# Weight preparation spread over 33 units, two blocks interleaved, and a rearranged chain after the last unit

## The chip, the core and the metric

The program runs on one core of a Trainium2 chip. The metric is the device time of one execution in microseconds. In what follows PE is the TensorE, DVE the VectorE, ACT the ScalarE, POOL the GpSimd and SP the queue from which all transfers here are issued.

## The reference

```python
x = block-causal attention of q, k, v          # 4 batches, 8 heads, 576 tokens, head size 64; blocks of 64
x = x.transpose(0, 2, 1, 3).reshape(2304, 512)
h = x @ w_in                                   # 512 -> 2048; w_in and w_out are float64 in memory
g = where(h >= 1, h, where(h <= -1, 0, (h + 1) ** 2 / 4))
y = g @ w_out                                  # 2048 -> 512
logits = y @ phi                               # 32 slots
d = softmax of logits over the 2304 tokens     # dispatch
s = d.T @ y                                    # 32 x 512, 4 slots to each of 8 experts
slot_out[e] = relu(s[e] @ w1[e]) @ w2[e]       # 512 -> 1024 -> 512
return (softmax of logits over the 32 slots) @ slot_out
```

All results are float32. The weights w1 and w2 of the experts are 33.6 MB together, the output is 4.7 MB.

## The kernel before, in words

There are three stages.

**Attention** (`attention`, `Pair`) handles 16 pairs of heads, one after another and overlapped, by the table PLAN. Its steps w0, w1 and w2 prepare the first READY = 6 of 16 tiles of w_in meanwhile, half a tile for each pair. The result x stays on the chip, in blocks of tokens BLK (512, 512, 512, 512, 256), blocks 0 and 1 already as a high and a low part, 2 to 4 as they are.

**The units** (`Moe.run`): unit (b, f) forms 128 columns f of h for block b, by 12 matmuls of 128x128 weights against 512 tokens (`h_unit`: high by high, high by low, low by high; 256 tokens in block 4), into one of three PSUM buffers of the pool ptr. Then `act_unit` forms the gate g; it is DVE's L520 that reads h last and so frees the buffer. The loop runs over 80 units k = 16 b + f. In unit k the tile READY + k is prepared as well, one a unit until 32 tiles are done (16 of w_in, 16 of w_out, in units 0 to 25): `w_raw` loads the float64 words, `w_mul` is an ACT pass (L422), `w_bits` four DVE passes (L428 to L431), `w_parts` POOL's work (L446 and L447 for w_in, the single addition L439 for w_out, which is then stored to DRAM, `wod`).

Beside this the table `sides` puts further steps behind a unit: `wo_turn` transposes a tile of w_out (PE L460, copied out by ACT), `wo_phi` and `wo_back` turn four of them into w2p = w_out phi; `quad` transposes four columns of g to gn (L534) and adds their logits (L540), each of the last in one of four 32-row groups of the array; `soft`, `disp`, `slots` and `weigh` do the softmax over tokens block by block, with a running maximum (`e.nm`) and scaled sums S. Each of these steps takes one of two PSUM buffers of the pool psc, or of ptr. `feed` issues 72 pieces of the experts' weights (32 of w1, 40 of w2) from SP as soon as one of 47 slots of 4 KB per partition (pools b4 and c4) is free by a plan, which a dry run of the same code makes.

**The end**: `chain` is the last quad, the softmax of block 4, the maximum and sums over all row groups (`maximum`, `weights`), the slots' inputs (`slots`, `turn`, `inputs`, `spread`); `tail` holds the experts' matmuls (`w1`, line L844; `w2`, line L871) and the output. The engines run each their instructions in the written order; a wait holds up everything behind it on its engine. `e.copy("A", ...)` is ACT, "D" is DVE.

Of the kernel before, what the change touches and what calls it, by code (L numbers as in the profile page):

```python
# [7 lines left out]
F32 = mybir.dt.float32  # L8
# [228 lines left out]
READY = 6  # L237
# [65 lines left out]
class Moe:  # L303


    BLK = [(0, 512), (512, 512), (1024, 512), (1536, 512), (2048, 256)]
    ASIDE = 2
    CAP = {"b4": 27, "c4": 20}

    def __init__(self, e, nc, live=None):  # L310
# [26 lines left out]
    def room(self, key):  # L337
# [46 lines left out]
    def split(self, i):  # L384

        n = self.BLK[i][1]
        for u in range(n // 256):
# [5 lines left out]
            yield one  # L393

# [57 lines left out]
    def wo_turn(self, f):  # L452
# [5 lines left out]
        ps = e.psc.tile([P, 2, 512], F32, tag="sc", name=f"wt{f}")[:, 0].rearrange("p (k c) -> p k c", k=4)  # L458
# [34 lines left out]
    def h_unit(self, b, f):  # L493
# [29 lines left out]
    def quad(self, b, q):  # L523
# [3 lines left out]
        nj = n // P  # L527
        fs = range(4 * q, 4 * q + 4)
        for u in range(nj // 2):
            ps = e.psc.tile([P, 2, 512], F32, tag="sc", name=f"gn{b}{q}{u}")  # L530
            for a in range(2):
                o = (2 * u + a) * P
                for i, f in enumerate(fs):
                    nc.tensor.transpose(ps[:, a, i * P:(i + 1) * P], self.gt(b, f)[:, o:o + P], e.ident)  # L534
            self.gn[b, q, u] = ps
        if q == 0:
            self.lt = e.ppv.tile([P, 512], F32, tag="pv", name=f"lt{b}")
# [4 lines left out]
        a = 1024 // n  # L542
        self.drop(*[f"g{b}_{f}" for f in fs if f % a == 0])
        for u in range(nj // 2):
            t = self.new([P, 2, 512], F32, f"gn{b}{q}{u}")
            e.copy("A", t, self.gn[b, q, u])
            self.gn[b, q, u] = t


    def soft(self, b):  # L550
        e, nc, sp = self.e, self.nc, self.e.sp
        R = self.BLK[b][1] // 4
        lt = self.lt[0:R, 0:P]
# [3 lines left out]
        nm, l = e.nm[0:R], e.l[0:R]  # L557
        if b == 0:
            nc.vector.tensor_reduce(out=nm, in_=lt, axis=AX.X, op=ALU.max, negate=True)
            nc.scalar.activation(E[0:R], lt, AF.Exp, bias=nm, accum_out=l)  # L560
        else:
            bm = sp.tile([P, 3], F32, tag="bm", bufs=2, name=f"bm{b}")
            f, rs = bm[0:R, 1:2], bm[0:R, 2:3]
            v["f"] = f
            nc.vector.tensor_reduce(out=bm[0:R, 0:1], in_=lt, axis=AX.X, op=ALU.max, negate=True)
            nc.vector.tensor_tensor(out=bm[0:R, 0:1], in0=bm[0:R, 0:1], in1=nm, op=ALU.min)
            nc.scalar.activation(E[0:R], lt, AF.Exp, bias=bm[0:R, 0:1], accum_out=rs)
            nc.scalar.activation(f, nm, AF.Exp, bias=bm[0:R, 0:1], scale=-1.0)
# [489 lines left out]
```

## Time and profile before

| | us |
|---|---|
| median of 2 runs | 561.64 (561.08 to 562.2) |
| the profiled execution | 561.42 |
| its span, first to last instruction | 559.6 |
| PE busy | 511.5 (91%) |
| DVE busy | 344.2 (62%) |
| ACT busy | 319.9 (57%) |
| POOL busy | 196.7 (35%) |
| read from and written to memory | 68.75 MB and 8.91 MB |

The span is what the rows cover; the execution lasts 1.8 us longer. Shares are means over stages with different limits, so rows are read by stage: attention to about 182 us, units from there to 489 us, of these the ones with preparation to about 300 us, then chain and tail.

### The profile page before, as it was taken

The numbers are of one execution on the slowest core, as the hardware profiler recorded it, in microseconds if no ns is written. First come the engines' busy times: TensorE is split into PE (matmuls) and PEld (weight loads), VectorE is DVE, ScalarE is ACT, GpSimd is POOL, SyncE is SP. The second block draws the span as 40 slices with busy tenths as digits, with TensorE's granted clock in tenths as the row PEclk, the third lists the DMA queues.
The fourth block names the chain that finished last, engine by engine and source line by source line (L and its number), as shares of the span: only waits on it lengthen the run. The fifth ranks groups of instructions, "written<-read, shape, count | busy, mean of one in ns | idle before, by whom it ended". The sixth has DMA issues, their size and how long they took to land.

```text
span 559.6 us, 11650 instructions
## 1 busy us (share of the span) xinstructions
PE 511.5 (91%) x4492; PEld 387.9 (69%) x4492; DVE 344.2 (62%) x679; ACT 319.9 (57%) x723; POOL 196.7 (35%) x255
## 2 busy tenths in 40 slices
PE   6899999999998976787989999999999999989995
PEld 5687777777776754565768867678868887943354
DVE  7799998997764899878652523344454446431232
ACT  5799988987863867577776433434324343320132
POOL 5888888887651566423220200003000100000000
PEclk8799999999999999999999999999999999989999
DMA  4542542523314522365520000142620059659998
GB/s 148 141 138 77 158 122 77 168 69 101 87 27 143 216 81 76 126 213 186 169 97 1 2 1 2 39 151 76 222 79 1 1 194 368 211 205 358 409 412 327
DMA packets 39542, 79.45 MB, mean 142 GB/s; under 512 B 8384, under 2 KB 17728, under 8 KB 39488
## 3 DMA queue, kind: packets, MB, share of 16 engines
q1 hardware_dynamic: 39488, 78.72, 41.3%
q8 instruction: 35, 0.57, 0.4%
q14 instruction: 19, 0.16, 0.1%
HBM read 68.75 MB, written 8.91 MB: 139 GB/s over the span
## 4 chain that ended last, share of the span: by engine, by line
PE 55%; DVE 22%; ACT 10%; issue 4%; DMA 3%; POOL 2%; SPq 0%; DVEq 0%; POOLq 0%; ACTq 0%
PE h L501 25%; PE gn L534 5%; ACT pr L147 5%; DVE wab L429 4%; DVE nm L142 3%; PE lt L540 3%; PE s L587 3%; DMA raw<-in_w_out_dram 3%; PE om L184 3%; PE eh L844 3%; PE acc L871 2%; DVE wab L428 2%; DVE PT L248 2%; DVE g L520 2%; DVE sm L152 1%
## 5 line engine op out<-in xcount | busy, mean ns | idle before, releaser
L501 PE MATMUL h<-xh,w 128*128 128x512 f32 (+1 forms) x384 | 108.9, 362 | 0.0
L501 PE MATMUL h<-xt,w 128*128 128x512 f32 x384 | 95.0, 398 | 13.0 <-DVE g L520 12.9
L158 POOL TENSOR_SCALAR pr<-pr,sm 128x384 f32<-128x384 f32 (+2 forms) x144 | 85.8, 614 | 22.0 <-DVE sm L153 10.5
L501 PEld LDWEIGHTS h<-xt,w 128*128 128x128 f32 x384 | 70.0, 188 | 31.5 <-DVE g L520 17.4
L519 DVE SCALAR_TENSOR_TENSOR ga<-ga 128x512 f32<-128x512 f32 (+1 forms) x52 | 34.2, 658 | 93.6 <-ACT ga L518 93.6
L518 ACT ACTIVATE ga<-h,half 128x512 f32<-128x512 f32 (+1 forms) x52 | 32.4, 622 | 97.0 <-PE h L501 96.2
L147 ACT ACTIVATE pr<-sc,nm 128x512 f32<-128x512 f32 (+2 forms) x144 | 79.0, 564 | 14.0 <-DVE nm L142 9.1
L501 PEld LDWEIGHTS h<-xh,w 128*128 128x128 f32 x384 | 68.5, 189 | 18.4 <-issue 8.0
L501 PE MATMUL h<-xl,w 128*128 128x512 f32 (+1 forms) x192 | 68.2, 355 | 0.0
L520 DVE TENSOR_TENSOR g<-h,ga 128x512 f32<-128x512 f32 (+1 forms) x80 | 51.0, 637 | 27.9 <-ACT ga L516 25.3
L614 POOL TENSOR_TENSOR cn<-cn,cm 128x128 f32<-128x128 f32 (+1 forms) x5 | 2.2, 442 | 186.2 <-DVE cm L613 186.2
L142 DVE TENSOR_REDUCE nm<-sc 128x2 f32<-128x1024 f32 (+1 forms) x64 | 51.7, 816 | 3.9 <-PE sc L123 3.5
L120 PE MATMUL sc<-K,Q 64*128 64x512 f32 (+3 forms) x384 | 47.2, 360 | 3.6 <-ACT pr L147 2.8
L246 ACT COPY gn<-gn 128x1024 f32<-128x1024 f32 x36 | 35.2, 1012 | 11.9 <-PE gn L534 10.5
L120 PEld LDWEIGHTS sc<-K,Q 64*128 64x128 f32 x384 | 29.8, 193 | 14.0 <-ACT pr L147 7.2
L501 PEld LDWEIGHTS h<-xl,w 128*128 128x128 f32 x192 | 36.3, 189 | 4.5
L534 PE MATMUL gn<-ident,g 128*128 128x128 f32 x288 | 35.5, 274 | 2.1 <-DVE g L520 1.2
L534 PEld LDWEIGHTS gn<-ident,g 128*128 128x128 f32 x288 | 32.1, 140 | 6.3 <-issue 1.7
L439 POOL TENSOR_TENSOR wab<-wab 128x512 f32<-128x512 f32 x16 | 20.5, 1282 | 44.2 <-DVE wab L431 41.8
L429 DVE SCALAR_TENSOR_TENSOR wab<-wab 128x512 uint32<-128x512 uint32 (+1 forms) x38 | 32.9, 865 | 2.2
L446 POOL TENSOR_TENSOR wab<-wab,w 128x256 f32<-128x256 f32 (+1 forms) x22 | 24.9, 1132 | 25.7 <-PE h L501 13.1
L422 ACT ACTIVATE wab<-raw 128x512 f32<-128x512 f32 (+1 forms) x38 | 22.7, 599 | 19.1 <-DMA raw<-in_w_out_dram 11.9
(192 smaller groups left out, 891.8 us busy)
## 6 DMA issues: line engine op xcount, KB each, us to landing
ew<-in_w_dram SPq DMA_DIRECT2D x32, 512.0 KB, 4.6
raw<-in_w_in_dram SPq DMA_DIRECT2D x16, 512.0 KB, 4.7
raw<-in_w_out_dram SPq DMA_DIRECT2D x16, 512.0 KB, 3.7
ew<-in_w2a_dram SPq DMA_DIRECT2D x16, 510.0 KB, 8.3
ew<-in_w2b_dram SPq DMA_DIRECT2D x16, 344.0 KB, 6.8
kn<-in_k_dram SPq DMA_DIRECT2D x16, 288.0 KB, 3.7
qn<-in_q_dram SPq DMA_DIRECT2D x16, 288.0 KB, 3.2
vn<-in_v_dram SPq DMA_DIRECT2D x16, 256.0 KB, 3.4
```

Source lines behind the costliest of these rows:

```text
L120: nc.tensor.matmul(sc[:, h, 0:n], self.Q[r, qa, 128 * i:128 * i + 128], self.K[r, ka, 0:n], start=(k == 0), stop=False)
L142: nc.vector.tensor_reduce(out=self.negm[:, 2 * i:2 * i + 2], in_=self.scs[i][:, :, 0:128 * (i + 1)], axis=AX.X, op=ALU.max, negate=True)
L147: self.nc.scalar.activation(pr, sc, AF.Exp, bias=self.negm[:, b:b + 1], accum_out=self.sums[:, b:b + 1])
L158: self.nc.gpsimd.tensor_scalar(out=pr, in0=pr, scalar1=self.sums[:, b:b + 1], scalar2=1.0, op0=ALU.mult, op1=ALU.mult)
L246: nc.scalar.copy(dst, src)
L429: v.scalar_tensor_tensor(out=Au, in0=Au, scalar=3, in1=Bu, op0=ALU.logical_shift_left, op1=ALU.bitwise_or)
L446: p.tensor_tensor(out=A, in0=A, in1=w[:, 0].bitcast(F32), op=ALU.subtract)
L501: nc.tensor.matmul(ph[:, 0:n], w[:, wi, kk], self.x(b, kk, xi)[:, 0:n], start=(m == 0), stop=(m == 11))
L518: nc.scalar.activation(ga, ph, AF.Relu, bias=e.half[:, 0:1], scale=0.5)
L519: nc.vector.scalar_tensor_tensor(out=ga, in0=ga, scalar=1.0, in1=ga, op0=ALU.min, op1=ALU.mult)
L520: nc.vector.tensor_tensor(out=g, in0=ph, in1=ga, op=ALU.max)
L534: nc.tensor.transpose(ps[:, a, i * P:(i + 1) * P], self.gt(b, f)[:, o:o + P], e.ident)
```

## The change

- READY is 7: pairs 13 and 14 carry half-tile preparations too.
- `VISITS` sets the order of units: columns 0 to 6 of block 0, 0 to 3 of block 1, then 7 to 15 of block 0, 4 to 15 of block 1, and blocks 2, 3, 4 as before.
- `plan_sides` replaces `sides`. The 25 tiles left are prepared at the units listed in `prep`, nine of w_in in units 0 to 14, sixteen of w_out in units 16 to 32; a tile is loaded two units ahead and turned two units behind.
- `wo_turn`, `wo_phi` and `wo_back` share one PSUM bank, `aside[:, 1]`, all copied out by ACT; phi and back stand within `h_unit`, after its ninth matmul. `aside` takes one of the two psc buffers for the first half of the units; its other bank holds the logits of block 1.
- `half` replaces `quad`: one half of it per unit, so 8 transposes at a time.
- The raw x of blocks 2 to 4 is stored to DRAM (`x_out`, units 2 and 3) and loaded again (`x_in`, units 27, 39, 55). The pool c4 has 21 slots, and `feed` leaves three slots free until the chain; it may start at unit 41.
- `widen` repeats w2p four times over columns, so that the logits of block 4 come out in all four row groups, by one 128-wide matmul of 256 columns per f.
- `maximum`, `weights` and a new `total`, which sums the row groups of S into T, run in units 68, 69 and 71. After the last unit remain `half`, `soft4`, `disp4`, `slots4` (8 matmuls), `turn` (4 transposes in place of 16 matmuls), `inputs` and `spread`; `sums` and `sums4` do in the tail what `total` and `total4` did.

```diff
 
-READY = 6
...
 
...
     ASIDE = 2
-    CAP = {"b4": 27, "c4": 20}
...
             return False
         k = 0
         for t in range(at, len(self.plan)):
...
+    def x_out(self, i, u):
+        self.nc.sync.dma_start(self.e.xd[:, 2 * i + u], self.xw[i, u].rearrange("p a n -> p (a n)"))
+        self.drop(f"xw{i}{u}")
...
+    def x_in(self, i, u):
+        n = self.BLK[i][1]
+        self.xw[i, u] = self.new([P, 1024 // n, n], F32, f"xw{i}{u}")
+        self.nc.sync.dma_start(self.xw[i, u].rearrange("p a n -> p (a n)"), self.e.xd[:, 2 * i + u])
...
-        ps = e.psc.tile([P, 2, 512], F32, tag="sc", name=f"wt{f}")[:, 0].rearrange("p (k c) -> p k c", k=4)
+        ps = self.aside[:, 1].rearrange("p (k c) -> p k c", k=4)
...
-        ps = e.psc.tile([P, 2, 512], F32, tag="sc", name=f"wphi{c}")[:, 0]
+        ps = self.aside[:, 1]
...
-        nc.vector.tensor_copy(wp, ps[:, 0:P])
+        nc.scalar.copy(wp, ps[:, 0:P])
...
-        ps = e.psc.tile([P, 2, 512], F32, tag="sc", name=f"wback{c}")[:, 0]
+        ps = self.aside[:, 1]
...
-        nc.vector.tensor_copy(e.w2p[:, 4 * c:4 * c + 4].rearrange("p i s -> p (i s)"), ps[:, 0:P])
+        nc.scalar.copy(e.w2p[:, 4 * c:4 * c + 4].rearrange("p i s -> p (i s)"), ps[:, 0:P])
...
+    def h_unit(self, b, f, mid=()):
...
+            if kk == 2:
+                for fn, *a in mid:
+                    getattr(self, fn)(*a)
...
+    def half(self, b, q, u):
...
+        ps = e.psc.tile([P, 2, 512], F32, tag="sc", name=f"gn{b}{q}{u}")
+        for j in range(2):
+            o = (2 * u + j) * P
+            for i, f in enumerate(fs):
+                nc.tensor.transpose(ps[:, j, i * P:(i + 1) * P], self.gt(b, f)[:, o:o + P], e.ident)
+        if u == n // 256 - 1:
+            self.logits(b, fs)
+            self.drop(*[f"g{b}_{f}" for f in fs if f % a == 0])
+        self.gn[b, q, u] = self.new([P, 2, 512], F32, f"gn{b}{q}{u}")
+        e.copy("A", self.gn[b, q, u], ps)
...
+    def logits(self, b, fs):
+        nc, lt = self.nc, self.lt[b]
         for f in fs:
-            for j in range(nj):
-                nc.tensor.matmul(self.lt[32 * j:32 * j + 32, 0:P], e.w2p[:, f], self.gt(b, f)[:, j * P:(j + 1) * P],
+            if b == 4:
+                nc.tensor.matmul(lt[:, 0:256], self.wide[f // 8][:, f % 8], self.gt(b, f), start=(f == 0), stop=(f == 15))
+                continue
+            for j in range(4):
+                nc.tensor.matmul(lt[32 * j:32 * j + 32, 0:P], self.e.w2p[:, f], self.gt(b, f)[:, j * P:(j + 1) * P],
                                  start=(f == 0), stop=(f == 15))
...
+        nc.vector.tensor_copy(nM[0:32, 4:5], ps[0:32, 0:1])
+        self.T = self.new([P, 512], F32, "T")
+        ps = e.psc.tile([P, 2, 512], F32, tag="sc", name="t_S")[:, 0]
+        for c in range(4):
+            nc.tensor.matmul(ps[32 * c:32 * c + 32], self.selw, self.S[c // 2][:, c % 2], start=True, stop=True)
+        self.drop("S0", "S1")
+        nc.scalar.copy(self.T, ps)
...
+    def widen(self, u):
+        t = self.wide[u] = self.new([P, 8, P], F32, f"wide{u}")
+        self.nc.gpsimd.tensor_copy(t.rearrange("p f (c s) -> p f c s", s=32),
+                                   self.e.w2p[:, 8 * u:8 * u + 8].unsqueeze(2).to_broadcast([P, 8, 4, 32]))
...
+    def soft4(self):
+        e, nc, sp = self.e, self.nc, self.e.sp
+        lt = self.lt[4][:, 0:256]
+        EL = self.EL
+        bm = self.bm = sp.tile([P, 3], F32, tag="bm", bufs=2, name="bm4")
+        nm, f, l = bm[:, 0:1], bm[:, 1:2], bm[:, 2:3]
+        nc.vector.tensor_reduce(out=nm, in_=lt, axis=AX.X, op=ALU.max, negate=True)
+        nc.vector.tensor_tensor(out=nm, in0=nm, in1=self.nM[:, 0:1], op=ALU.min)
+        nc.scalar.activation(EL[0:32, 0], lt[0:32], AF.Exp, bias=nm[0:32], accum_out=l[0:32])
+        nc.scalar.activation(f, self.nM[:, 0:1], AF.Exp, bias=nm, scale=-1.0)
+        nc.scalar.copy(EL[0:32, 1], lt[0:32])
...
+        ps = e.psc.tile([P, 2, 512], F32, tag="sc", name="s4")[:, 0]
+        for j in range(2):
+            for c in range(4):
+                nc.tensor.matmul(ps[32 * c:32 * c + 32], self.EL[:, 2, 32 * j:32 * j + 32], self.gn[4, c, 0][:, j],
+                                 start=(j == 0), stop=(j == 1))
+        self.drop(*[f"gn4{c}0" for c in range(4)])
+        for o in (0, 256):
+            T = self.T[:, o:o + 256]
+            nc.vector.scalar_tensor_tensor(out=T, in0=T, scalar=self.bm[:, 1:2], in1=ps[:, o:o + 256],
+                                           op0=ALU.mult, op1=ALU.add)
...
-        for i in range(8):
-            nc.tensor.matmul(ps[:, i], self.S[r][:, i // 4, i % 4 * P:(i % 4 + 1) * P], self.selw, start=True, stop=True)
-        self.drop(f"S{r}")
-        e.copy("AD"[r], self.sg[:, 8 * r:8 * r + 8].rearrange("p f s -> p (f s)"), ps.rearrange("p f s -> p (f s)"))
+        ps = e.ptr.tile([P, 512], F32, tag="tr", name=f"t_s{r}")[:, 0:256]
+        for i in range(2):
+            t = 2 * r + i
+            nc.tensor.transpose(ps[:, i * P:(i + 1) * P], self.T[:, t * P:(t + 1) * P], e.ident)
+        e.copy("AD"[r], self.sg[:, 2 * r:2 * r + 2].rearrange("p t c -> p (t c)"), ps)
...
+        for t in (2 * r, 2 * r + 1):
+            for c in range(4):
+                f = 4 * c + t
+                nc.tensor.matmul(self.si[32 * c:32 * c + 32], self.sg[:, t, 32 * c:32 * c + 32], self.wo[f // 2][:, f % 2],
+                                 start=(t == 0), stop=(t == 3))
+        self.drop(*[f"wo{2 * c + r}" for c in range(4)])
...
+        prep = [i * 7 // 4 for i in range(first)] + [16 + i * 6 // 5 for i in range(6)] + [23 + i for i in range(10)]
...
+            k = put(prep[first + f] + 2, "wo_turn", f)
...
+                put(-k - 3, "wo_back", c)
+                free = k + 3
+                for b in range(2):
+                    for u in range(2):
+                        free = put(max(free + 1, pos[b, f] + 2), "half", b, c, u)
...
+                if b == 2:
+                    put(3, "x_out", b, u)
+                    put(pos[b, 0] - 5, "x_in", b, u)
+                else:
+                    put(2, "x_out", b, u)
+                    put(pos[b, 0] - 9, "x_in", b, u)
+                put(pos[b, 0] - (3 if b == 2 else 6) + u, fn)
...
+        units = [(b, f) for b, f0, f1 in self.VISITS for f in range(f0, f1)]
...
+        self.aside = e.psc.tile([P, 2, 512], F32, tag="sc", name="aside")
+        self.lt = {1: self.aside[:, 0]}
...
+            for i in [READY + n for n, p in enumerate(prep) if p == k - 1]:
+                self.w_parts(i)
+            for i in [READY + n for n, p in enumerate(prep) if p == k]:
+                self.w_mul(i)
                 self.w_bits(i)
...
+            for i in [READY + n for n, p in enumerate(prep) if max(p - 2, 0) == k and n > 1]:
+                self.w_raw(i)
...
-            if k > 50:
+            if k > 40:
...
-        e = self.e
-        self.sg = self.new([P, 16, 32], F32, "sg")
-        for step in (lambda: self.quad(4, 3), lambda: self.soft(4), self.maximum, lambda: self.disp(4), lambda: self.comb(0),
-                     self.weights, lambda: self.slots(4, 0), lambda: self.slots(4, 1), lambda: self.comb(1),
+        self.sg = self.new([P, 4, P], F32, "sg")
+        self.half(4, 3, 0)
+        self.drop("wide0", "wide1")
+        for step in (self.soft4, lambda: self.comb(0), self.disp4, lambda: self.comb(1), self.slots4,
                      lambda: self.turn(0), lambda: self.turn(1), lambda: self.inputs(0), lambda: self.inputs(1), self.spread):
             step()
             self.feed()
```

Three places show how instructions move. On DVE, the stretch with units 3 to 5; L428 to L431 (now L439 to L442) prepare a tile, L520 (now L534) forms g, which frees h. Before:

```order
L520 TENSOR_TENSOR g_2_2917<-h_3_2935,ga_3_2948 128x512
L428 TENSOR_SCALAR wab_2931<-raw_2902 128x512
L429 SCALAR_TENSOR_TENSOR wab_2931<-wab_2931 128x512
L430 TENSOR_SCALAR wab_2931<-wab_2931 128x512
L431 SCALAR_TENSOR_TENSOR wab_2931<-raw_2902,wab_2931 128x512
L520 TENSOR_TENSOR g_4_2978<-h_4_2965,ga_4_2979 128x512
L428 TENSOR_SCALAR wab_2961<-raw_2933 128x512
L429 SCALAR_TENSOR_TENSOR wab_2961<-wab_2961 128x512
L430 TENSOR_SCALAR wab_2961<-wab_2961 128x512
L431 SCALAR_TENSOR_TENSOR wab_2961<-raw_2933,wab_2961 128x512
L520 TENSOR_TENSOR g_4_2978<-h_5_2996,ga_5_3009 128x512
```

Now:

```order
L534 TENSOR_TENSOR g_2_2929<-h_3_2946,ga_3_2959 128x512
L534 TENSOR_TENSOR g_4_2983<-h_4_2970,ga_4_2984 128x512
L439 TENSOR_SCALAR wab_2989<-raw_2944 128x512
L440 SCALAR_TENSOR_TENSOR wab_2989<-wab_2989 128x512
L441 TENSOR_SCALAR wab_2989<-wab_2989 128x512
L442 SCALAR_TENSOR_TENSOR wab_2989<-raw_2944,wab_2989 128x512
L534 TENSOR_TENSOR g_4_2983<-h_5_2997,ga_5_3010 128x512
L534 TENSOR_TENSOR g_6_3034<-h_6_3021,ga_6_3035 128x512
```

Units 4 and 6 carry no tile any more. On PE, the change's rows around the second part of `wo_phi` and `wo_back` (units 23 to 25; the `aside` rows are L480 phi, L489 back, L471 turn):

```order
L480 MATMUL aside<-wT_3416,phi 32x128 x2
L512 MATMUL h_7_3492<-xt_147,w_2882 128x512 x3
L512 MATMUL h_8_3538<-xt_144,w_2912 128x512 x3
L512 MATMUL h_8_3538<-xt_145,w_2912 128x512 x3
L512 MATMUL h_8_3538<-xt_146,w_2912 128x512 x3
L489 MATMUL aside<-ident,wp_3518 128x128
L512 MATMUL h_8_3538<-xt_147,w_2912 128x512 x3
L471 MATMUL aside<-ident,wab_3449 128x128 x4
L512 MATMUL h_9_3574<-xt_144,w_2966 128x512 x3
```

Each `aside` row writes the same bank, and three or nine matmuls of h stand between the last two pairs of them. On PE again, what follows the last unit. Before:

```order
L540 MATMUL lt_5444<-g_12_5594,w2p 32x128 x8
L622 MATMUL t_m<-ident,nm 1x128
L577 MATMUL et_5712<-ident,E_5696 128x64
L820 MATMUL ct_5716<-identr,n_5458 128x128 x4
L631 MATMUL t_b<-ones,row 128x2
L587 MATMUL s_5729<-gn_5453,en_5714 32x512 x2
...
L820 MATMUL ct_5749<-identr,n_5463 128x128 x4
L658 MATMUL t_s_5755<-selw,S_4160 128x32 x8
L658 MATMUL t_s_5767<-selw,S_4226 128x32 x8
```

Now:

```order
L560 MATMUL lt_5447<-g_12_5610,wide_5076 128x256 x4
L920 MATMUL ct_5719<-identr,n_5467 128x128 x4
L690 MATMUL et_5726<-ident,EL 128x32 x2
L920 MATMUL ct_5730<-identr,n_5467 128x128 x4
L698 MATMUL s_5736<-gn_5461,EL 32x512
...
L712 MATMUL t_s_5755<-ident,T 128x128 x2
L712 MATMUL t_s_5759<-ident,T 128x128 x2
```

The two rows for the maximum have left this place, and the 16 small matmuls are 4 transposes.

## Rows read from the trace of the kernel before

**Rows 1.** Busy time by stretch: start:end, length, each engine, PE clock, DMA share, GB/s.

```profile
182.00:300.00 118.00, 95.39 (x584) 73.90 (x583) 90.95 (x132) 85.31 (x135) 49.67 (x36) 1.00 0.40 138
300.00:489.00 189.00, 187.90 (x1539) 148.91 (x1538) 84.41 (x155) 73.09 (x114) 14.89 (x10) 1.00 0.28 99
```

**Rows 2.** PE's waits from 182 to 489 us: line, releaser, total us, times, longest.

```profile
PE h L501 <- DVE g L520: 12.9, 10, 1.3
PE wt L460 <- ACT wT L246: 4.1, 4, 1.7
PE wt L460 <- ACT gn L246: 3.3, 2, 1.9
PE wback L478 <- DVE wp L473: 2.3, 1, 2.3
```

**Rows 3.** Timeline of a unit that prepares w_in: start, us, engine, line, operation, tiles.

```profile
219.30 0.68 DVE L520 TENSOR_TENSOR g<-h,ga 128x512 f32<-128x512 f32 x1
220.04 3.04 PE L501 MATMUL h<-xt,w 128*128 128x512 f32 x12 [1.29 <-DVE g L520]
220.84 1.67 DVE L429 SCALAR_TENSOR_TENSOR wab<-wab 128x512 uint32<-128x512 uint32 x1
223.61 0.68 DVE L520 TENSOR_TENSOR g<-h,ga 128x512 f32<-128x512 f32 x1
```

**Rows 4.** Timeline of units that prepare w_out.

```profile
268.56 0.69 DVE L429 SCALAR_TENSOR_TENSOR wab<-wab 128x512 uint32<-128x512 uint32 x1
271.66 0.60 PE L460 MATMUL wt<-ident,wab 128*128 128x128 f32 x4
```

**Rows 5.** Timeline of DVE in attention: one row of each pair, the same step.

```profile
113.82 0.73 DVE L140 TENSOR_REDUCE nm<-sc 128x1 f32<-128x576 f32 x1
124.12 0.73 DVE L140 TENSOR_REDUCE nm<-sc 128x1 f32<-128x576 f32 x1
143.52 0.73 DVE L140 TENSOR_REDUCE nm<-sc 128x1 f32<-128x576 f32 x1
153.48 0.73 DVE L140 TENSOR_REDUCE nm<-sc 128x1 f32<-128x576 f32 x1
```

**Rows 6.** Timeline of PE: logits of block 4, sums of block 3, one wide matmul.

```profile
464.88 1.92 PE L587 MATMUL s<-gn,en 128*32 128x512 f32 x16
478.60 1.07 PE L540 MATMUL lt<-g,w2p 128*32 128x128 f32 x16
538.85 0.84 PE L890 MATMUL t_o<-hN,sel 128*128 128x340 f32 x2
```

**Rows 7.** The chain of waits from the last unit on: start, us, what.

```profile
487.48 1.64 PE h L501 x12
490.59 0.77 PE gn L534 x5
492.98 0.46 ACT E L567 x2
495.34 5.25 PE s L587 x16
501.06 3.56 PE t_s L658 x32
504.63 3.62 PE si L668 x32
510.80 7.05 PE eh L844 x60
546.95 1.35 PE acc L871 x32
```

**Rows 8.** Busy time by stretch again, in two short ones.

```profile
515.00:525.00 10.00, 9.79 (x92) 3.20 (x88) 1.38 (x2) 1.25 (x3) 0.00 (x0) 1.00 1.03 410
495.00:497.00 2.00, 2.00 (x8) 0.72 (x10) 0.45 (x3) 0.84 (x2) 0.00 (x0) 0.61 0.00 0
```

**Rows 9.** The page's DMA issues: tiles, queue, count, size of one, us from issue to landing.

```profile
ew<-in_w_dram SPq DMA_DIRECT2D x32, 512.0 KB, 4.6
```

More of the change, by code (lines that the diff above doesn't have):

```diff
@@ L233 @@
 WARM = 44
-READY = 6
+READY = 7
 def attention(e, tc, nb=4, wl=(1, 1 + 2 * READY)):
@@ L520, in act_unit @@
         nc.vector.tensor_tensor(out=g, in0=ph, in1=ga, op=ALU.max)
-    def quad(self, b, q):
+    def half(self, b, q, u):
         e, nc = self.e, self.nc
         n = self.BLK[b][1]
-        nj = n // P
+        a = 1024 // n
         fs = range(4 * q, 4 * q + 4)
[L529 to L537, printed above, removed]
-        for f in fs:
-            for j in range(nj):
-                nc.tensor.matmul(self.lt[32 * j:32 * j + 32, 0:P], e.w2p[:, f], self.gt(b, f)[:, j * P:(j + 1) * P],
-                                 start=(f == 0), stop=(f == 15))
[L542 to L547, printed above, removed]
@@ new lines, in disp4, with slots4 @@
+    def disp4(self):
+        e, nc = self.e, self.nc
+        ps = e.ptr.tile([P, 512], F32, tag="tr", name="et4")
+        for j in range(2):
+            nc.tensor.transpose(ps[:, 32 * j:32 * j + 32], self.EL[0:32, 0, j * P:(j + 1) * P], e.ident[0:32, 0:32])
+        nc.vector.tensor_copy(self.EL[:, 2, 0:64], ps[:, 0:64])
+    def slots4(self):
+        e, nc = self.e, self.nc
+        ps = e.psc.tile([P, 2, 512], F32, tag="sc", name="s4")[:, 0]
+        for j in range(2):
+            for c in range(4):
[6 more added lines that the diff above has]
+                                           op0=ALU.mult, op1=ALU.add)
@@ L694, in put @@
             return k
-        first = 16 - READY
         for f in range(16):
-            k = put(first + f + 3, "wo_turn", f)
+            k = put(prep[first + f] + 2, "wo_turn", f)
             if f % 4 == 3:
-                put(k + 2, "wo_phi", f // 4)
-                back = put(k + 3, "wo_back", f // 4)
-                free = put(max(back + 1, f + 2), "quad", 0, f // 4)
-        for b in range(4):
+                c = f // 4
+                put(-k - 2, "wo_phi", c)
+                put(-k - 3, "wo_back", c)
[3 more added lines that the diff above has]
+                        free = put(max(free + 1, pos[b, f] + 2), "half", b, c, u)
+        for b in range(2):
+            put(free + 2 * b, "soft", b)
+            put(free + 2 * b + 1, "disp", b)
+            put(free + 2 * b + 2, "slots", b, 0)
+            put(free + 2 * b + 3, "slots", b, 1)
+            put(free + 2 * b + 2, "weigh", b)
+        free += 2
+        for b in range(2, 4):
+            for q in range(4):
+                for u in range(2):
+                    free = put(max(free + 1, pos[b, 4 * q + 3] + 2), "half", b, q, u)
             put(free, "soft", b)
@@ L707, in sides @@
             put(free + 4, "weigh", b)
[L708 to L710 removed]
+        put(free + 2, "maximum")
+        put(free + 3, "weights")
+        put(free + 5, "total")
         for q in range(3):
[L712 removed]
+            put(pos[4, 4 * q + 3] + 3, "half", 4, q, 0)
         for b in range(2, 5):
             for u, fn in enumerate(self.split(b)):
[L715 removed]
+                if b == 2:
+                    put(3, "x_out", b, u)
+                    put(pos[b, 0] - 5, "x_in", b, u)
+                else:
+                    put(2, "x_out", b, u)
+                    put(pos[b, 0] - 9, "x_in", b, u)
+                put(pos[b, 0] - (3 if b == 2 else 6) + u, fn)
         for u in range(8):
[L717 to L718 removed]
+            put(44 + u, "wo_load", u)
+        put(56, "widen", 0)
+        put(58, "widen", 1)
+        return at, prep
     def run(self):
@@ L935, in tail @@
         w1(0)
-        self.total()
+        self.sums()
         w1(1)
```

132 lines of the change are left out of this document (64 added, 68 removed).

## The prediction

> **What bounds the kernel now.** I read the busy time by stretch first [rows 1]. While tiles are still prepared, from 182 to 300 us, PE is busy for 95.4 of 118 us; from 300 to 489 us it is busy for 187.9 of 189. So the units lose 22.6 us, all in the first stretch, and after 300 us only PE's own work counts. PE's waits say what ends that idle time [rows 2]: 12.9 us until DVE's gate has freed a PSUM buffer of h, ten times about 1.3 us, and 9.7 us in seven waits for a copy out of a PSUM buffer in which w_out is turned. They add up to 22.6, the same number. The timeline shows the first kind [rows 3]: from gate to gate DVE takes 223.61 - 219.30 = 4.31 us where a tile of w_in is prepared, the matmuls of the unit 3.04. After unit 79 it is the chain that sets the end [rows 7]: its last matmul ends at 487.48 + 1.64 = 489.12, and the experts' matmuls begin at 510.80, 21.7 us later. Meanwhile the weight stream stands still (DMA share 0.00 in 495 to 497 us), and then runs at 410 GB/s [rows 8], the share of 16 engines at 1.03: full.
>
> The sum is made against the profiled execution, 561.42 us, with a span of 559.6 and 1.8 us around it; the median shown is 561.64, the same within 0.05%.
>
> **The preparation.** Nine w_in tiles now stand in units 0 to 14, so that DVE needs 9 x 4.31 us and 6 gates of 0.68, 42.9 us, where PE needs 15 x 3.04 = 45.6. DVE no longer sets the pace over the stretch. A unit's lead survives one prepared neighbour, since h has three buffers; where two tiles are neighbours before a lead is there (units 0 and 1), I charge the old wait twice, 2 x 1.27 = 2.5 us. That is also my price of everything left, bounds 0 and 10: the upper end is eight waits of the 1.3 us in rows 2. Sixteen w_out tiles stand in units 16 to 32. Their DVE pass L429 takes 0.69 us, against 1.67 in a w_in unit [rows 3, 4]; with three passes that are no longer than in rows 3 and the gate that is at most 4.31 - 0.98 = 3.33 us, against 3.04 + 0.60 of matmuls and a turn on PE [rows 3, 4]. PE leads, and with halves of gn beside it more so. All turns, phis and backs write one bank, so each must find ACT's copy of the one before done. Between two of them stand at least three matmuls of h, mostly nine or twelve, 0.76 to 3.04 us [rows 3], against a copy that ended the old waits after 1.7 us at most [rows 2]. Loads are issued two units ahead instead of about one. So the gain is 22.6, less 2.5.
>
> The steps that went from DVE to ACT (the eight copies of phi and back) cost nothing where PE does not wait for them; behind them are the three gate passes of their unit, and the matmuls of the next unit are their cover. If that cover were gone it would be the 1.4 us a hand-over of rows 2.
>
> **Attention.** Two more pairs carry preparation. Where a pair has it, the period is 124.12 - 113.82 = 10.30 us; without, 153.48 - 143.52 = 9.96 [rows 5]. Two pairs: +0.7 us (bounds 0 and 1).
>
> **x through DRAM.** Five stores of 0.52 MB and five loads pass SP, the stores ahead of the tile loads of units 2 and 3. DMA is busy 0.40 and 0.28 of the time in these stretches [rows 1]; the 5.2 MB take 13 us at 410 GB/s [rows 8], spread over 55 units. Behind them on SP only loads wait that are used two units later. Priced at 0, upper end 5 us (a rival, below).
>
> **Logits of block 4.** Now 4 matmuls of 256 columns on the whole array, before 8 narrow ones in two of its four row groups, 1.07 us [rows 6]. The sums of block 3 put 16 passes of 512 columns through in 1.92 us with four groups at once, that is 0.94 ns per column and pass on one group; 8 passes of 256 columns are 1.9 us. The wide matmul nearest to it, two passes of 340 columns in 0.84 us, gives 4 x 0.84 x 256/340 = 2.5. I take 1.9, since the second row holds the filling of the array once in each; +0.83 a quad, three quads before the last unit ends: +2.5 us (0 to 4.3).
> The Trainium skill has a rule that speaks against this edit: TensorEngine Tiling (Array Packing), section Theoretical Speedup, gives up to 4x for a stationary operand of at most 32 columns, which the change gives up. Two groups were in use, so it says up to twice 1.07 us, an estimate of +3.2 in place of +2.5, and 544.1 us at the end; the two prices from rows 6 lie on either side of it.
>
> **Steps moved into the units.** `maximum`, `weights` and `total` keep PE for two tiny operations and four matmuls of 512 columns in four groups: half of the 1.92 us of rows 6, 0.96. With the tiny ones, 1.5 us (1 to 2.5). The DVE and ACT parts lie in a stretch where DVE is busy for 84 of 189 us [rows 1]; a transpose that waits for one costs PE nothing, since the next unit stands ahead of it.
>
> So the last unit ends at 489.1 - 22.6 + 2.5 + 0.7 + 2.5 + 1.5 = **473.7 us**.
>
> **Chain and tail.** On PE the chain loses 3.56 us of t_s (now four transposes, about 0.6), half of the sums and the steps for the maximum [rows 7]; the experts' matmuls could begin some 15 us after the last unit instead of 21.7. I don't book these 6.5 us, because of the stream. `feed` keeps three slots free until the chain, so the order of SP holds 26 pieces ahead of it, before 29. Three more go out as the chain begins, one after the logits, and pieces 30 to 71 wait until `slots4` has read gn. When that is: 1.47 us from the last matmul to the first transpose behind the gate (490.59 - 489.12), 0.77 of transposes, 1.9 of logits, 1.3 for the maximum and the exponential (from 491.36 to 493.44 before, less 1.07 of logits, plus 0.3 for twice the columns), 0.7 for the transpose and its copy, 1.92 for the sums [rows 6, 7]: 8.1 us. At 495 to 497 us, 6 us after the last unit, the granted clock was 0.61, half the time at the lower of its two levels [rows 8], and the sums took 5.25 us [rows 7]. At that level the last step doubles: 10.0. I take 9.3. From there 2 pieces of 0.524 MB and the 16.78 MB of w2 remain, 17.8 MB: 43.5 us at 410 GB/s, plus the first landing, 4.6 us [rows 9] less the 1.3 that one piece takes anyway, 3.3. The last piece is then used in 0.5 us, and what followed the last of these matmuls before, 559.6 - 548.30 = 11.3 us [rows 7], follows again. 9.3 + 43.5 + 3.3 + 0.5 + 11.3 = **67.9 us**, against 559.6 - 489.1 = 70.5 before. Six and a half on PE turn into 2.6, the rest is late weights.
>
> Sum: 473.7 + 67.9 = 541.6 of span, + 1.8: **543.4 us**, 3.2% less.
>
> **Rivals.**
> *One bank as the bound (slower).* All 24 hand-overs of `aside[:, 1]` pass an ACT copy. ACT has in these units the three gate passes, the next tile's first pass, the copy of the turn and, from unit 25, that of a half of gn. If the copies come after the next unit's matmuls, PE waits at each: the row for seven such waits is 9.7 us, 1.4 each [rows 2]. Twenty-four times that would be 33.6 in place of 2.5, 574.5 us. It decides when ACT's work in a unit exceeds PE's. For it: seven waits exist already with two buffers. Against it: half of them were behind copies of a whole quad, 1.9 us at most, which are now halves, and ACT was busy for 85 of 118 us [rows 1]. It needs nearly every hand-over to fail. Chance 0.05.
>
> *DVE and POOL in each other's way.* A w_in tile's L429 takes 1.67 us where POOL works beside it, a w_out tile's 0.69 [rows 3, 4]. If POOL's addition or its splitting of x falls on DVE's passes in the new order, the w_out units go at up to 4.31 us where PE has 3.64, and seven of them (16 to 22, before halves are on PE) lose 0.7 each, and the w_in units lose their slack, 2 us more: +7, 550 us. The Trainium skill, SBUF — State Buffer, section Who interferes with whom, calls the port pair that these two engines share an exclusive lock; the two durations of L429 agree with it. Chance 0.13.
>
> *The stream does not set the end.* If the slots come free earlier, the chain's gain is kept: 15 us and then the 559.6 - 510.8 = 48.8 that followed before [rows 7], so 473.7 + 63.8 + 1.8 = 539.3 us. For it: the sums may run at the full clock (S at 8.1), and other slots are free. Against it: the full DMA share of rows 8. Chance 0.14.
>
> *Reloaded x is late, or the three spare slots bring other waits.* x of block 2 is loaded at unit 27 and needed at 32, with two splits on POOL between; late by one unit it costs up to 5 us, 548.5. Chance 0.1.
>
> *It does not do what it says:* DVE's gate still frees h late in the first units as in all ten waits of rows 2, +10, 551. Chance 0.08. My forecast keeps 0.5.
>
> **How the numbers follow.** A difference of 2% is about what a measurement tells from none: faster is under 550.4, slower over 572.9. The forecast, the third, the fourth and most of the second rival lie below 550.4: 0.5 + 0.14 + 0.1 + 0.08 = 0.82 faster; the rest of the second, the last, and half-failing hand-overs 0.14 within 2%; 0.04 slower. The range of 537.5 to 551 reaches from the stream not binding with cheap logits (539.3 less 2) to the last rival, and takes in the bounds of the residual waits; it leaves out the slow case and some of the mixed ones.
>
> **What would show it.** PE busy in the units with preparation close to the stretch's length, with h <- DVE waits under 4 us in all; waits of `aside` rows for ACT near zero (rival one: over 20 us); L439 to L442 as short in w_out units as now (rival two: a second pass over 1.5 us there); lt of block 4 near 1.9 us; the last unit ending near 474; DMA share near 1 from some 10 us after it until the last pieces, with PE's last weight matmuls waiting for DMA. A gain in the tail of over 5 us, or none, would make the prediction of that part wrong.

## The result, and the profile after

The changed kernel took 542.29 us (541.03 to 543.55, 2 runs), 0.9655 of before (95% interval 0.9551 to 0.976); predicted were 543.4 us. Later, beside other kernels, it took 541.52, 0.9636 of before (0.961 to 0.9662). The profiled execution lasted 541.03 us, its span 539.2, predicted 541.6.

Busy time by stretch, with the columns of [rows 1]; the units now end at 470.7 us:

```profile
182.00:290.00 108.00, 105.72 (x653) 85.54 (x655) 83.13 (x123) 96.44 (x154) 47.66 (x34) 1.00 0.49 175
290.00:471.00 181.00, 178.38 (x1469) 140.45 (x1462) 82.36 (x155) 71.31 (x115) 14.50 (x12) 1.00 0.32 110
```

To 290 us PE loses 2.3 us (before, to 300 us, 22.6), and 2.6 from there to the last unit (before 1.1). Its waits in the units, all that the view lists (before: [rows 2]):

```profile
PE s L601 <- DVE en L594: 2.3, 1, 2.3
PE aside L480 <- ACT wT L246: 1.9, 3, 1.1
PE aside L471 <- POOL wab L450: 0.2, 1, 0.2
PE aside L489 <- ACT wT L246: 0.2, 1, 0.2
```

The wait for DVE's gate is gone. Four hand-overs of the bank by ACT cost 2.1 us, one wait for POOL's w_out tile 0.2, and one wait is new: 2.3 us for `en` of block 1. PE's timeline says the same of the first units, and shows the end of that wait:

```profile
179.47 52.37 PE L512 MATMUL h<-xt,w 128*128 128x512 f32 x228
...
353.17 1.92 PE L601 MATMUL s<-gn,en 128*32 128x512 f32 x16 [2.27 <-DVE en L594]
```

On the timeline of all engines, POOL and DVE ahead of it:

```profile
348.02 2.40 POOL L393 TENSOR_TENSOR xl<-xw,xh 128x1024 fp32r<-128x1024 f32 x1 [1.93 <-ACT xh L392]
348.57 2.40 DVE L533 SCALAR_TENSOR_TENSOR ga<-ga 128x512 f32<-128x512 f32 x1 [1.41 <-ACT ga L532]
```

PE's first row is 19 units, 228 matmuls, without a pause: 2.76 us each, where a unit between pauses took 3.04 [rows 3].

DVE's passes have become shorter too. Its second pass, L440, of a w_in tile that stands alone, and of a w_out tile beside POOL's split of block 2's x (POOL's L393 is busy from 280.56 to 282.96 us):

```profile
192.71 0.69 DVE L440 SCALAR_TENSOR_TENSOR wab<-wab 128x512 uint32<-128x512 uint32 x1
281.05 2.47 DVE L440 SCALAR_TENSOR_TENSOR wab<-wab 128x512 uint32<-128x512 uint32 x1 [0.98 <-ACT wab L433]
```

It takes 0.69 us in seven of nine w_in tiles and 1.60 in two (before, as L429, 1.67 in nine of ten). Of the sixteen w_out tiles two are long: 2.47 us beside that split, and 1.58 beside POOL's addition of the tile before.

The chain of waits from the last unit on (before: [rows 7]):

```profile
469.30 1.44 PE h L512 x12
...
472.97 1.74 PE lt L560 x8
...
476.83 1.95 PE s L698 x16
...
485.18 9.78 DMA ew<-in_w2a_dram
...
519.45 6.77 DMA ew<-in_w2b_dram
...
526.26 0.54 PE acc L971 x8
```

The chain that ended last runs from `spread` to the last weight matmul over DMAs, not over PE as before. PE's own waits for pieces make only 1.8 us of it (six, on L971). And the rows by stretch beside it:

```profile
477.00:479.00 2.00, 1.68 (x16) 0.26 (x8) 0.12 (x1) 0.45 (x1) 0.00 (x0) 1.00 0.42 172
490.00:500.00 10.00, 9.78 (x92) 3.13 (x88) 1.38 (x2) 1.20 (x2) 0.00 (x0) 1.00 1.03 412
```

The clock stayed at 1.00 through the sums, where before it fell to 0.61 [rows 8].

### The profile page after: what moved, and what is told of

Read it like the earlier page. It is cut to its first block, busy times and chain, and to the rows that moved or that the text cites. A ratio compares the mean times of both kernels' runs of the same rounds, so it can differ in the third digit from the quotient of the medians.

```text
span 539.2 us, 11594 instructions
## 1 busy us (share of the span) xinstructions
PE 507.1 (94%) x4442; PEld 386.2 (72%) x4442; DVE 334.7 (62%) x670; ACT 329.1 (61%) x742; POOL 198.8 (37%) x261
## 4 chain that ended last, share of the span: by engine, by line
PE 58%; DVE 15%; ACT 11%; DMA 8%; issue 2%; POOL 1%; DVEq 0%; SPq 0%; ACTq 0%
PE h L512 32%; ACT pr L147 6%; PE gn L549 5%; DMA ew<-in_w2a_dram 5%; DVE nm L142 3%; PE om L184 3%; DMA ew<-in_w2b_dram 2%; PE lt L563 2%; PE s L601 2%; DVE PT L248 2%; PE sc L120 1%; PE sc L113 1%; PE lt L560 1%; DVE sm L152 1%; ACT PT L246 1%
## 5 line engine op out<-in xcount | busy, mean ns | idle before, releaser
L512 PE MATMUL h<-xh,w 128*128 128x512 f32 (+1 forms) x384 | 112.9, 366 | 0.0
L512 PE MATMUL h<-xt,w 128*128 128x512 f32 x384 | 92.1, 395 | 0.0
L533 DVE SCALAR_TENSOR_TENSOR ga<-ga 128x512 f32<-128x512 f32 (+1 forms) x47 | 30.9, 658 | 88.6 <-ACT ga L532 88.6
L512 PEld LDWEIGHTS h<-xh,w 128*128 128x128 f32 x384 | 68.7, 189 | 13.5 <-issue 2.8
L532 ACT ACTIVATE ga<-h,half 128x512 f32<-128x512 f32 (+1 forms) x47 | 28.9, 615 | 72.1 <-PE h L512 71.3
L512 PE MATMUL h<-xl,w 128*128 128x512 f32 (+1 forms) x192 | 68.1, 355 | 0.0
L534 DVE TENSOR_TENSOR g<-h,ga 128x512 f32<-128x512 f32 (+1 forms) x80 | 50.9, 637 | 19.5 <-ACT ga L530 16.8
L246 ACT COPY gn<-gn 128x1024 f32<-128x1024 f32 x36 | 36.4, 1011 | 13.6 <-PE gn L549 13.6
L549 PE MATMUL gn<-ident,g 128*128 128x128 f32 x288 | 37.7, 273 | 1.2 <-DVE g L534 1.2
L457 POOL TENSOR_TENSOR wab<-wab,w 128x256 f32<-128x256 f32 (+1 forms) x23 | 23.3, 1012 | 30.7 <-ACT w L246 16.4
L393 POOL TENSOR_TENSOR xl<-xw,xh 128x1024 fp32r<-128x1024 f32 x5 | 12.0, 2410 | 59.5 <-ACT xh L392 58.7
L440 DVE SCALAR_TENSOR_TENSOR wab<-wab 128x512 uint32<-128x512 uint32 (+1 forms) x39 | 27.8, 712 | 7.0 <-ACT wab L433 3.5
```

What stands on the lines that cost most here:

```text
L246: nc.scalar.copy(dst, src)
L440: v.scalar_tensor_tensor(out=Au, in0=Au, scalar=3, in1=Bu, op0=ALU.logical_shift_left, op1=ALU.bitwise_or)
L457: p.tensor_tensor(out=A, in0=A, in1=w[:, 0].bitcast(F32), op=ALU.subtract)
L532: nc.scalar.activation(ga, ph, AF.Relu, bias=e.half[:, 0:1], scale=0.5)
L533: nc.vector.scalar_tensor_tensor(out=ga, in0=ga, scalar=1.0, in1=ga, op0=ALU.min, op1=ALU.mult)
L534: nc.vector.tensor_tensor(out=g, in0=ph, in1=ga, op=ALU.max)
```

## The experiments

From each trace: the start of the first unit, the end of the last, PE's idle time between them (pauses over 0.1 us), the rest of that time (work at the granted clock), and from the last unit to the end of the span.

| kernel | first unit | last ends | idle | rest | tail | span | ratio to before (interval) |
|---|---|---|---|---|---|---|---|
| before | 178.9 | 489.1 | 23.7 | 286.5 | 70.5 | 559.6 | 1 |
| the change | 179.5 | 470.7 | 4.9 | 286.4 | 68.5 | 539.2 | 0.9636 (0.961 to 0.966) |
| one tile a unit | 179.5 | 483.2 | 14.5 | 289.1 | 68.1 | 551.3 | 0.984 (0.982 to 0.986) |
| old unit order | 180.5 | 483.7 | 11.8 | 291.4 | 68.3 | 552.0 | 0.984 (0.982 to 0.986) |
| phi, back behind | 179.3 | 481.2 | 11.1 | 290.8 | 68.4 | 549.6 | 0.984 (0.981 to 0.987) |
| READY 6 | 178.8 | 475.3 | 7.7 | 288.8 | 70.2 | 545.4 | 0.974 (0.972 to 0.977) |
| zeros behind spread | 179.8 | 471.0 | 5.0 | 286.2 | 68.7 | 539.7 | 0.964 (0.961 to 0.967) |
| zeros before slots4 | 180.6 | 473.4 | 5.0 | 287.9 | 72.2 | 545.6 | 0.972 (0.970 to 0.975) |
| four narrow groups | 179.5 | 473.5 | 5.0 | 289.0 | 68.4 | 542.0 | 0.965 (0.962 to 0.968) |
| split earlier | 179.7 | 468.5 | 2.7 | 286.1 | 68.4 | 536.9 | 0.957 (0.955 to 0.960) |
| groups, split, two slots | 180.6 | 470.4 | 2.7 | 287.1 | 68.1 | 538.5 | 0.958 (0.956 to 0.961) |
| split, slots earlier | 180.6 | 469.3 | 2.6 | 286.1 | 65.3 | 534.6 | 0.954 (0.952 to 0.956) |

**The change once more.**

> The changed kernel itself, for a narrower interval beside the two above: 539 to 540 of span, ratio 0.962 to 0.967.

Span 539.0, 541.52 us: as expected, and the second row of the table takes its ratio from here.

**One tile a unit.**

```diff
-        prep = [i * 7 // 4 for i in range(first)] + [16 + i * 6 // 5 for i in range(6)] + [23 + i for i in range(10)]
+        prep = list(range(25))
```

> One edit to the changed kernel (539.2 us of span): the 25 tiles are prepared one a unit, in units 0 to 24, as before the change; turns stay two units behind and in the one bank, units in the new order. Theory (spacing ended the wait for DVE's gate): nine neighbouring w_in units at 4.3 us of DVE against 3.0 of PE bring back some nine waits h <- DVE g of 1.3 us, 10 to 13 us more, the last unit ends near 482 us and the span is 549 to 552. Rival (the hand-overs of the turned tiles and the unit order made the gain, the spacing nothing): under 2 us more.

The last unit ends 12.5 us later, as the theory had it. The wait for DVE's gate is back, seven times; the other wait, of a turn for POOL's tile, is not one of before:

```profile
PE h L512 <- DVE g L534: 9.1, 7, 1.3
PE aside L471 <- POOL wab L450: 2.8, 4, 2.0
```

Idle time grew by 9.6 (the wait for `en` is not there), the rest by 2.8, at a clock of 1.00 in each stretch of the units and with the same matmuls: a pause costs PE more than the idle time that the profile shows. And DVE's second pass is long again, beside POOL's work on the tile before, in eight of the nine w_in tiles:

```profile
195.71 1.60 DVE L440 SCALAR_TENSOR_TENSOR wab<-wab 128x512 uint32<-128x512 uint32 x1
```

So spacing does two things: it gives a tile's DVE work nearly two units of PE, and it moves POOL's work on the tile before away from its second pass. From gate to gate a spaced tile takes DVE 194.51 - 191.37 = 3.14 us, where the sum has 4.31. How much each is worth no run tells apart. The edit also moves a part of the gate from ACT to DVE eight units earlier, from unit 25 on, behind all seven of these waits.

**Old unit order.**

```diff
-    VISITS = [(0, 0, 7), (1, 0, 4), (0, 7, 16), (1, 4, 16), (2, 0, 16), (3, 0, 16), (4, 0, 16)]
+    VISITS = [(0, 0, 16), (1, 0, 16), (2, 0, 16), (3, 0, 16), (4, 0, 16)]
```

> One edit to the changed kernel: the units of block 0 and 1 in their old order, preparation as spread as now. Theory (the four units of block 1 put ahead only give the last w_in tiles time): tile 15 is prepared in unit 14 and needed in unit 15, so PE waits for w <- POOL two or three times, 2 to 6 us more, 541 to 545 of span. Rival 1 (order does nothing): within 1 us. Rival 2 (without it each tile is late): over 10 us.

The last unit ends 13.0 us later (1.0 of it before the first unit): the theory's place, the second rival's size. The waits are for a tile of w, as named, but four, 7.2 us. The rest is 5.0 us longer, most of it where the granted clock was lower. After three of the waits within 10 us, and only 0.76 us of work from 225 to 230 us, it was:

```profile
230.00:235.00 5.00, 4.58 (x11) 3.63 (x12) 0.00 (x0) 0.00 (x0) 0.36 (x1) 0.50 0.01 3
```

11 matmuls in 5 us, where the same kernel ran 23 from 210 to 215 us at 1.00: 0.50 is the lower of the two levels (1.2 of 2.4 GHz). The sums behind the wait for `en` took 3.20 us here, in place of 1.92 (below).

**Phi and back behind their unit.**

```diff
-                put(-k - 2, "wo_phi", c)
-                put(-k - 3, "wo_back", c)
+                put(k + 2, "wo_phi", c)
+                put(k + 3, "wo_back", c)
```

> One edit to the changed kernel: wo_phi and wo_back stand behind their unit, directly ahead of that unit's turn or half, no longer inside after the ninth matmul. Theory (the one bank is only harmless where matmuls stand between its users): six pairs of neighbours wait for ACT's copy, 1.0 to 1.7 us each, 5 to 10 us more, in waits of aside rows for ACT. Rival (ACT is free enough, the place does not matter): under 1.5 us.

The last unit ends 10.4 us later. Idle time grew by 6.2: three new waits after back, 5.1 us, and others of 1.2 us behind phi and 2.0 at a half, where 1.9 us of phi's own waits are gone. One of the three, behind back at 251.84 us:

```profile
251.84 0.27 PE L489 MATMUL aside<-ident,wp 128*128 128x128 f32 x1
254.44 0.63 PE L471 MATMUL aside<-ident,wab 128*128 128x128 f32 x4 [2.33 <-ACT w2p L490]
```

So the single bank is harmless only with matmuls between its users. The other 4.4 us lie mostly where the granted clock was lower: 0.66 from 280 to 285 us and 0.73 from 295 to 300, each behind waits of over 2 us, and 0.71 from 360 to 365, behind the wait for `en`.

**READY 6.**

```diff
-READY = 7
+READY = 6
```

> One edit to the changed kernel: READY is 6 again, so attention carries 12 half tiles and the units 26 tiles, ten of w_in in units 0 to 15. Theory (DVE has 10 x 4.31 + 6 x 0.68 = 47.2 us there against about 16 x 2.75 = 44 of PE): attention 0.7 us less, one or two waits h <- DVE g more, 0 to 3 us more in all. Rival (the seventh tile is what makes the spacing hold): 5 us more.

6.2 us more of span: neither account. The first unit starts 0.7 us earlier. No wait for DVE's gate appears, since seven of the ten w_in tiles have the short second pass; idle time grew by 2.8, of which a turn waits 2.1 us for POOL. The rest grew by 2.5, of which 1.6 are the sums behind the wait for `en`, 3.51 us at a lower clock. The tail grew by 1.7: 29 weight pieces were issued when slots4 was done, 30 in the change. The size is near the rival's 5 us, the way to it is not the rival's.

**Zeros behind spread, and zeros before slots4.** The same 70 matmuls at two places, where they delay what follows them on PE by 3.9 and 4.0 us.

```diff
-                     lambda: self.turn(0), lambda: self.turn(1), lambda: self.inputs(0), lambda: self.inputs(1), self.spread):
+                     lambda: self.turn(0), lambda: self.turn(1), lambda: self.inputs(0), lambda: self.inputs(1), self.spread,
+                     lambda: self.fill(self.e.ptr.tile([P, 512], F32, tag="tr", name="fill")[:, 0:P], 70)):
```

In the second kernel the same step stands ahead of `self.slots4`:

```diff
-        for step in (self.soft4, lambda: self.comb(0), self.disp4, lambda: self.comb(1), self.slots4,
+        for step in (self.soft4, lambda: self.comb(0), self.disp4, lambda: self.comb(1),
+                     lambda: self.fill(self.e.ptr.tile([P, 512], F32, tag="tr", name="fill")[:, 0:P], 70), self.slots4,
```

> One edit to the changed kernel: 70 matmuls of zeros, about 4 to 5 us of PE, between spread and the experts' first matmul, so that PE reaches the weights later while the slots that the chain frees come free as before. Theory (the weight stream sets the end): under 1 us more, and PE's waits for the last pieces shrink by the time that the matmuls take. Rival (PE's work sets the end): 4 to 5 us more.

> One edit to the changed kernel (539.2 us of span): the 70 matmuls of zeros, 3.9 us of PE, stand ahead of slots4 instead of behind spread. Theory (the stream sets the end, and pieces 30 and later wait until slots4 has read gn): the matmuls that cost 0.5 us behind spread cost 3.5 to 4 us here, 542.7 to 543.3 of span. Rival (the stream has enough to do before, the slots of slots4 are not what it waits for): under 1.5 us.

Tail 68.7 and 72.2 us, the change's own 68.5 and 68.1 in two profiles. 3.9 us of PE cost 0.2 behind spread, and 3.7 ahead of slots4. The stream sets the end, and slots4 sets the stream. The margin is used up by it: from the first matmul of the experts to the last PE takes 41.2 us in the change and 37.4 with the zeros behind spread, where no wait for a piece is left. So the profile shows 1.8 us of waits where PE had 3.8 to spare. (The second kernel's span has 2.7 us more from its first unit's start and from the clock, below.)

**Four narrow groups.**

```diff
-                nc.tensor.matmul(lt[:, 0:256], self.wide[f // 8][:, f % 8], self.gt(b, f), start=(f == 0), stop=(f == 15))
+                for c in range(4):
+                    nc.tensor.matmul(lt[32 * c:32 * c + 32, 0:256], self.e.w2p[:, f], self.gt(b, f), start=(f == 0), stop=(f == 15))
...
-        put(56, "widen", 0)
-        put(58, "widen", 1)
```

> One edit to the changed kernel: the four copies of block 4's logits come from four narrow matmuls of 32 columns a piece in the four row groups, with w2p itself; widen and its two slots of SBUF go, so two more weight pieces are issued ahead of the chain (28, before 26). PE: 16 narrow matmuls in four groups at once, about 1.9 us a quad by the sums' row, against 1.73 wide: 0 to +0.8 in all. Theory (what counts is when slots4 frees the slots of piece 30 on): no gain from the two pieces, span 538.8 to 540.2. Rival (what counts is how many pieces are ahead): 2.5 us less, 536.5 to 537.5.

The tail is 68.4 us, unchanged with two more pieces ahead of the chain: piece 29 has landed when slots4 is done, and 30 is issued only then, as in the change. The span, 542.0, is above the range, and the units have the difference: the sums behind the wait for `en` took 3.62 us. A quad's logits took 1.86 us, wide 1.73. (A narrow matmul's rows show `128*32`, rows by columns of the array: what the texts on record call row groups are groups of its columns.)

**Split earlier.**

```diff
-                    put(pos[b, 0] - 9, "x_in", b, u)
-                put(pos[b, 0] - (3 if b == 2 else 6) + u, fn)
+                    put(pos[b, 0] - (12 if b == 3 else 9), "x_in", b, u)
+                put(pos[b, 0] - (3 if b == 2 else 9 if b == 3 else 6) + u, fn)
```

> One edit to the changed kernel: block 3's x is loaded and split three units earlier (units 36, 39, 40 instead of 39, 42, 43). In the changed kernel DVE's pass L533 takes 2.40 us instead of 0.68 beside POOL's subtraction of that split, and PE then waits 2.27 us for en. Theory (POOL holds DVE up there): that wait goes, 2 to 2.5 us less, 536.7 to 537.3 of span. Rival (the softmax steps alone are too close): within 0.7 us.

The wait for `en` is gone, 2.3 us of span less. POOL is not all of the reason. From the end of `et` to `en` DVE took 3.0 us longer in the change than here, of which 1.7 is L533's longer pass; the gate also began 1.3 us later, behind ACT's pass L392 of the same split, 1.05 us. The edit moves both, and no run parts them.

The wait could cost more than its length: in five of the kernels of the table (old order, phi and back behind, READY 6, zeros before slots4, four groups) the sums behind it took 3.2 to 3.6 us, in both profiles of the change and with zeros behind spread 1.92. The row in the kernel with zeros before slots4, and the clock behind it:

```profile
354.26 3.37 PE L601 MATMUL s<-gn,en 128*32 128x512 f32 x16 [2.27 <-DVE en L594]
```

```profile
356.00:358.00 2.00, 2.00 (x10) 0.44 (x3) 0.30 (x1) 0.00 (x0) 0.00 (x0) 0.50 0.00 0
```

**Groups, split, two slots.** Both edits above, and:

```diff
-                self.hN = self.new([P, 2, 512], F32, "hN")
-                self.st = self.new([P, 1024], F32, "st")
-                nc.gpsimd.memset(self.st, 0.0)
...
         self.drop(*[f"gn4{c}0" for c in range(4)])
+        self.st = self.new([P, 1024], F32, "st")
+        nc.gpsimd.memset(self.st, 0.0)
...
+        self.hN = self.new([P, 2, 512], F32, "hN")
         comb_parts(order[2])
```

> The changed kernel with both edits above (four narrow groups, split three units earlier) and two slots allocated later: st behind slots4, hN in the tail. 30 pieces are issued ahead of the chain, 34 after slots4 (before 26 and 33). Theory: the split gives 2.3 us; the stream has piece 31 and one more done when slots4 frees the rest, 1.3 to 2.5 us; span 534.3 to 535.6. Rival (the end does not hang on slots): 537.

Span 538.5, outside both accounts. The tail is 68.1, and of the 1.3 to 2.5 us nothing clear came: the change's own two profiles have 68.5 and 68.1. Pieces up to 30 had landed by 474 us, and the stream stood still until slots4. From slots4 to the last piece it took 46.7 us in place of 47.5; the steps before and behind that took 0.5 more.

**Split, slots earlier.** The split as above; `later` allocates sg and st, and clears st; hN is allocated in the tail, `spare` is 1.

```diff
-        self.sg = self.new([P, 4, P], F32, "sg")
         self.half(4, 3, 0)
...
-        for step in (self.soft4, lambda: self.comb(0), self.disp4, lambda: self.comb(1), self.slots4,
-                     lambda: self.turn(0), lambda: self.turn(1), lambda: self.inputs(0), lambda: self.inputs(1), self.spread):
+        for step in (self.soft4, self.disp4, self.slots4, self.later,
+                     lambda: self.turn(0), lambda: self.turn(1), lambda: self.inputs(0), lambda: self.inputs(1),
+                     lambda: self.comb(0), lambda: self.comb(1), self.spread):
```

> The changed kernel with the earlier split of block 3's x (2.3 us less in the units, as measured) and slots freed for the stream ahead of slots4: sg and st are allocated behind slots4, hN in the tail, the two combs stand behind the slots' inputs, one spare slot in place of three; the logits stay wide. 33 pieces are issued before slots4 has read gn (30 in the change, 31 in the last trial), 35 right after it. Theory (the stream is full from slots4 on, so each piece already landed then is 1.1 to 1.3 us less): up to 3.8 us less in the tail, of which PE's own work (about 64 us after the last unit) leaves some 3: span 533 to 534.5. Rival (the pieces ahead only move the standstill): 536 to 537.

536.12 us (535.55 to 536.4), where the change took 541.52 beside it; the span is 534.6, 0.1 above the theory's range. The tail is 65.3, 3.2 less than the change's. The moved combs did little of it: slots4 is done 7.8 us after the last unit, 8.0 in the change. The pieces did the rest: at that moment 31 had landed and two more were under way, the next landed 1.5 us later, and the stream took 44.7 us from slots4 to its last piece. In the kernel above 31 had landed but none was under way, the next landed after 3.5 us, and it took 46.7; in the change it was 29 and one under way, and 47.5. PE is back on the chain, to 521 us:

```profile
485.48 7.00 PE eh L946 x64
...
518.84 1.30 PE acc L973 x32
```

## Why the prediction was right, point by point

The last unit ended at 470.7 us (forecast 473.7) and the tail took 68.5 (67.9). The mechanism of both parts is shown, but several terms were off and cancel, so that the total lies this close is partly luck.

- **Preparation**, 22.6 less 2.5: idle time fell from 23.7 to 4.9 us, 18.8. What is left is not what I charged: no wait at units 0 and 1, but 2.3 us at the bank and for POOL, and the 2.3 us for `en`, where I had put such a wait only into the rival on reloaded x, and there for another reason. Spacing, unit order and the places of phi and back are each needed; with any one undone the last unit ends 10 to 13 us later. And the comparison that carried this term held by luck: fifteen unbroken units take PE 15 x 2.76 = 41.4 us, not 45.6, which is less than the 42.9 that I gave DVE. No wait for the gate came because most spaced tiles' second pass no longer ran beside POOL: 9 x 3.14 + 6 x 0.68 = 32.3 us, an estimate that leaves out the two longer tiles. I had not foreseen that.
- **A term was missing.** The work added (logits, moved steps) is 3.4 us, yet PE's time without idle is the same, 286.4 after 286.5. A unit that starts after a pause takes 3.04 us, one in an unbroken row 2.76. I read 3.04 as the unit's cost; 0.28 of it goes with each pause, by the profile's modelled ends of matmuls. PE paused 21 times before (over 0.1 us) and 8 times after; thirteen times 0.28 is 3.6, an estimate that covers the missing 3.4. The first experiment shows it backwards: nine more pauses, and the rest grew by 2.8 with the same matmuls.
- **Attention** +0.7: the first unit starts 0.6 later. The eleven profiles with READY 7 have it at 179.3 to 180.6, the two with READY 6 at 178.8 and 178.9, so the sign holds and the size cannot be told closer than 0.3 to 1.9.
- **Logits** +2.5: 1.73 against 1.07 three times, 2.0. The Trainium skill's rule, TensorEngine Tiling (Array Packing), section Theoretical Speedup, made it 2.14, an estimate; the trace decides for less.
- **Moved steps** +1.5: 1.4 us of PE.
- **Tail** 67.9: 68.5. slots4 was done 8.0 us after the last unit, not 9.3, since the clock stayed up; the stream took 47.5 us from there to its last piece, against 46.8; and from that landing to the end 13.0, against 11.8. Six output transfers, issued while the last pieces were on their way, land up to 7.9 us behind the last of them, and five more behind these. It was 13.0 before as well (546.7 to 559.6); I had counted from the last matmul instead of the last landing. That -1.3, +0.7 and +1.2 nearly cancel is luck.
- **The stream does not set the end** had 539.3 us, and the measured 541 to 542 lie between it and the forecast. The time alone does not decide; the two kernels with zeros do. PE could begin the experts 14.9 us after the last unit (forecast 15), 6.8 sooner than before, and 2.0 of that reached the end.
- **DVE and POOL in each other's way**: the sign that I named, a second pass over 1.5 us in w_out units, came twice, 2.47 and 1.58 us, yet PE lost no time to DVE there, so the rival's mechanism showed and its price did not. A collision cost PE time at one place that I had not priced, L533's 2.40 us beside POOL's L393 of 2.40, the one ending at 351.0 and the other at 350.4 us; moving the split took the wait away, with ACT's part of it. The Trainium skill, SBUF — State Buffer, section Who interferes with whom, has the exclusive lock that fits this row.
- **Two readings** in the prediction are wrong and do not move the sum. A granted clock of 0.61 between levels of 0.50 and 1.00 is the lower level for about three quarters of the time, not half. And of the seven waits of rows 2 that are no waits for the gate, two are behind a quad's copy, not half of them.

## What to carry to other kernels

Price a pause of PE by the difference of periods, not by the idle time that the profile shows: here 4.31 less 2.76, 1.55 us for each wait of 1.3, and more where the clock falls behind it. Look what runs beside a long pass before you take its length as given: DVE's tile took 4.31 us beside POOL and 3.14 spaced. When a stream of weights sets the end, find the instruction that frees the slots it waits for. Work ahead of it cost its full length here, work behind it next to nothing, up to the 3.8 us that PE had to spare; and more pieces ahead paid only where some were still under way when it was done, so that the stream did not stand still. Spacing one engine's work over twice the units helped only with the order of use and the buffers' hand-overs moved along.

## What had not been expected of the hardware

The same pause of 2.27 us, ahead of the same instructions, was followed by the clock's lower level in five kernels (sums of 3.20 to 3.62 us; granted clock 0.50 in the row shown) and not in the two others that have it (1.00, 1.92 us, the change in both of its profiles). What decides it stays open.
